# A gated recurrence with a highway layer behind it: two units' gate values stored as pairs of neighbouring tokens

## The chip, the cores and the metric

The kernel runs on one core of a Trainium2 chip. TensorE (PE, with its weight loads shown apart as PEld), VectorE (DVE), ScalarE (ACT) and GpSimd (POOL) work side by side, each through its own instructions in order; SyncE (SP) issues the loads and stores. The metric is the time of one execution on the device in microseconds (us). A profiled execution also gives a span, from its first to its last instruction.

## The reference

Two layers, one behind the other, over 4 sequences of 6336 tokens with 256 channels (25344 tokens in all):

```python
sig = 1.0 / (1.0 + np.exp(-f_logit))
f = lower_bound + (1.0 - lower_bound) * sig
i = 1.0 - f
for t in range(S):                       # a recurrence along each sequence
    h = f[:, t] * h + i[:, t] * x[:, t]
    y[:, t] = h
# y as (25344, 256) is the x of the second layer:
H = np.maximum(x @ w_h, 0.0)
T = 1.0 / (1.0 + np.exp(-(x @ w_t + b_t)))
out = T * H + (1.0 - T) * x
```

## The kernel before, in words

The tokens are cut into 29 **units** of 256, 512 or 1024 tokens (`parts`: two of 2 blocks of 128, three of 4, twenty-two of 8, one of 4, one of 2). Units 10 and 12, which the change touches, have 8 blocks, so 1024 tokens. A unit is loaded with 128 partitions, each holding 8 neighbouring tokens with their 256 channels in float32. The channels are worked in two halves of 128.

The order of the work is written out by hand: `order` is a list of tokens such as `f10.0v:0`, which are issued one after the other. The letter is the step, the first number the unit, the second the half (or piece), `v` puts a step on DVE that else runs on ACT or POOL, and the number behind the colon is the buffer. Each engine runs its instructions in that order. The steps of one unit are:

- `l`, `x`: loads of the logits and of `x`, 1 MB each for a large unit, from SP's queue.
- `u` (ACT): u = sigmoid(-logit), in float16, one instruction of 128x2048 for a whole unit. `u` is kept as [partition, token, channel], and there are four buffers.
- `b` (POOL, in a few places DVE): `bv` = u * x, bfloat16, for one half of the channels, stored as **pairs**: [partition, pair of tokens, channel, token in the pair], so that two neighbouring tokens of one channel share a 4-byte word. There are eight buffers.
- `i` (PE): `u` turned to channels x tokens, into one PSUM bank (`uT`), by one 128x128 transpose for each of the 8 blocks (float16). The bank is then ordered [token in the partition, partition].
- `f` (ACT, or DVE with `v`): f = 1 + ncc * uT, from PSUM to SBUF in float16. It puts the tokens in their order in time, and so reads the bank with a hop of 128 values at each step. Among the large units only `f10.0` and `f12.1` run on DVE.
- `p` (PE): `bv` turned in the same way, but as 4 transposes of 4-byte words: each word holds a pair. The results are written at a step of 4 words, so that the bank is in the order of time.
- `s` (DVE): the recurrence, one scan of 1024 steps for each half.
- `g`, `z` (PE): the two products with the weights; `t` (ACT): the sigmoid of `z`; `d` (DVE): the maximum, from `y` and `g`; `e` (POOL or DVE): d = d * t.
- `o` (PE): output and transposition back into PSUM; `c` (ACT, sometimes DVE): copy to SBUF; `w`: store from SP's queue.

PSUM banks are shared: slots `a0` and `a1` (one bank each) hold `uT` and `bT` in turn, slots `b0` to `b2` (two banks each) hold `g`, `z` and `op` in turn. A step that fills a bank waits until the step that empties the one before has ended. `shared` adds a wait to a POOL product: it doesn't start before the last DVE product of its kind has ended.

Of the kernel before, what the change touches and what calls it, by code (L numbers as in the profile page):

```python
# [11 lines left out]
FP32 = mybir.dt.float32  # L12
BF16 = mybir.dt.bfloat16
FP16 = mybir.dt.float16
AF = mybir.ActivationFunctionType
# [4 lines left out]
def kernel(  # L20
# [10 lines left out]
    nc = tc.nc  # L31
    B, S, D = x.shape
    assert (B, S, D) == (4, 6336, 256)
    P = 128
    NH = D // P
    NB = 8
# [7 lines left out]
    units, at = [], 0  # L44
# [50 lines left out]
w28.1 c28.0:1 w28.0  # L95
"""

    NU = len(units)
    pool = ctx.enter_context(tc.tile_pool(name="sb", bufs=1))
    ps = ctx.enter_context(tc.tile_pool(name="ps", bufs=1, space=bass.MemoryType.PSUM))  # L100

    st = [dict() for _ in range(NU)]
    once = {}
    pin = tc.keep_in_program_order

    def sb(shape, dtype, name, slot=0):
        return pool.tile(shape, dtype, tag=f"{name}{slot}", name=name)
# [19 lines left out]
    def one_bank(slot, dtype, name):  # L127
        t = ps.tile([P, NB * P], dtype, tag=f"a{slot}", name=name)
        busy(t.bitcast(FP32))
        return t  # L130
# [10 lines left out]
    ident_h = sb([P, P], FP16, "ident_h")  # L141
    make_identity(nc, ident_h)
    ident_f = sb([P, P], FP32, "ident_f")
# [19 lines left out]
    def tokens(n):  # L163
        return units[n][0] * P
# [10 lines left out]
    def shared(ins, gpsimd):  # L175

        if not gpsimd:
            held[:] = [ins]
        elif held:
            tc.add_manual_dep(ins.ins, held.pop().ins.name, mybir.DependencyInfo(  # L180
                mybir.DependencyClass.Sync, mybir.DependencyReason.DATA), reason="shared port")
# [80 lines left out]
    def do_u(n, k, eng, slot):  # L262
        nb = units[n][0]
        u = sb([P, NB, D], FP16, "u", slot)
        pin(nc.scalar.activation(u[:, :nb], st[n]["l"][:, :nb], AF.Sigmoid, scale=-1.0))  # L265
        st[n]["u"] = u

    def do_b(n, h, eng, slot):
        nb = units[n][0]
        bv = sb([P, NB // 2, P, 2], BF16, "bv", slot)  # L270
        own = slice(h * P, (h + 1) * P)
        e = nc.vector if eng else nc.gpsimd
        shared(pin(e.tensor_mul(bv[:, :nb // 2].rearrange("p k d j -> p k j d"),  # L273
                                st[n]["u"][:, :nb, own].rearrange("p (k j) d -> p k j d", j=2),
                                st[n]["x"][:, :nb, own].rearrange("p (k j) d -> p k j d", j=2))), not eng)
        st[n]["bv", h] = bv

    def do_i(n, h, eng, slot):
        uT = one_bank(slot, FP16, "uT")
        for j in range(units[n][0]):  # L280
            pin(nc.tensor.transpose(uT[:, j * P:(j + 1) * P], st[n]["u"][:, j, h * P:(h + 1) * P], ident_h))  # L281
        st[n]["uT", h] = uT

    def do_f(n, h, eng, slot):
        N, nb = tokens(n), units[n][0]
        f = sb([P, NB * P], FP16, "f", slot)
        to = f[:, :N].rearrange("c (p j) -> c p j", j=nb)
        of = st[n]["uT", h][:, :N].rearrange("c (j p) -> c p j", j=nb)
        if eng:
            pin(nc.vector.tensor_scalar(to, of, ncc[:, h:h + 1], 1.0, op0=ALU.mult, op1=ALU.add))  # L290
        else:
            pin(nc.scalar.activation(to, of, AF.Identity, scale=ncc[:, h:h + 1], bias=1.0))  # L292
        st[n]["f", h] = f
# [103 lines left out]
    for token in order.split():  # L397
        token, _, slot = token.partition(":")
# [6 lines left out]
        n, _, k = name[1:].partition(".")  # L405
# [29 lines left out]
```

## Time and profile before

| | before |
|---|---|
| time | 206.22 us, median of 2 runs (205.97 to 206.46) |
| profiled execution | 205.65 us, span 203.9 us |
| instructions | 4594 |
| busy, share of the span | ACT 95%, DVE 94%, PE 92%, POOL 85% |
| moved by DMA | 78.68 MB, mean 386 GB/s |
| granted TensorE clock | 0.996 |

The profile divides the span among engines and groups of instructions; a group has its source line, engine, operation, the names of output and inputs with their shape, the count, the busy time and the mean length of one. Idle time is put down to what ended it. The timeline lists instructions with start and length. On ACT, DVE and POOL an instruction can start before the end of the one ahead of it is recorded, so the spacing of starts is shorter than the lengths.

### The profile page before, as it was taken

How to read it: one execution, taken by the hardware profiler on the slowest of the kernel's cores; microseconds unless marked ns; L12 is line 12 of the kernel's file. 1: busy time of each engine (PE TensorE's matmuls, PEld its weight loads, DVE VectorE, ACT ScalarE, POOL GpSimd, SP SyncE). 2: the span in 40 equal slices, each digit the busy share in tenths (PEclk: the TensorE clock that was granted, in tenths of full speed). 3: DMA queues.
4: the chain of work that ended last, by engine and by line, in shares of the span. 5: the costliest groups of instructions: out<-in, count | busy, mean ns of one | idle time of the engine just before them, and what ended most of it. 6: DMA issues, size and time to landing. Idle time of an engine off the chain costs nothing.

```text
span 203.9 us, 4594 instructions
## 1 busy us (share of the span) xinstructions
PE 187.5 (92%) x1794; PEld 131.9 (65%) x1820; DVE 192.6 (94%) x162; ACT 194.2 (95%) x203; POOL 172.8 (85%) x96
## 2 busy tenths in 40 slices
PE   7888869899999989999999999899999999999991
PEld 2455556566766755786668577667767667786880
DVE  2899989999999999999999999999999999999991
ACT  4899999999999999999999999999999999998991
POOL 3147988989999999999999959999999999788720
PEclk9999999999999999999999999999999999999998
DMA  6999999999999999999999999996999999579696
GB/s 213 367 420 424 416 418 423 409 420 422 418 426 416 423 424 417 420 419 424 417 423 420 427 416 416 427 419 273 336 341 411 420 416 399 209 289 367 272 372 251
DMA packets 16413, 78.68 MB, mean 386 GB/s; under 512 B 1796, under 2 KB 2568, under 8 KB 10760
## 3 DMA queue, kind: packets, MB, share of 16 engines
q1 hardware_dynamic: 16384, 78.39, 95.3%
q8 instruction: 14, 0.23, 0.5%
q14 instruction: 7, 0.06, 0.1%
q10 hardware_dynamic: 8, 0.00, 0.0%
HBM read 52.43 MB, written 25.95 MB: 384 GB/s over the span
## 4 chain that ended last, share of the span: by engine, by line
PE 47%; POOL 13%; ACT 12%; DMA 11%; DVE 7%; issue 5%; SPq 1%; ACTq 0%; POOLq 0%; DVEq 0%
DMA x<-in_x_dram 11%; POOL bv L273 8%; PE op L377 7%; PE op L378 7%; PE z L332 6%; PE g L332 6%; PE uT L281 6%; POOL d L355 6%; PE bT L301 5%; DVE y L320 5%; PE z L112 5%; PE g L112 5%; ACT o L390 4%; ACT t L345 3%; ACT f L292 3%
## 5 line engine op out<-in xcount | busy, mean ns | idle before, releaser
L273 POOL TENSOR_TENSOR bv<-u,x 128x1024 bf16<-128x1024 f16 (+2 forms) x53 | 103.7, 1981 | 15.9 <-DVE d L355 7.7
L320 DVE TENSOR_TENSOR_SCAN y<-f,y,bT 128x1024 bf16<-128x1024 f16 (+5 forms) x56 | 107.4, 1929 | 1.1 <-ACT f L292 0.9
L355 POOL TENSOR_TENSOR d<-d,t 128x512 bf16<-128x512 bf16 (+3 forms) x30 | 68.1, 2279 | 6.3 <-ACT t L345 3.6
L349 DVE SCALAR_TENSOR_TENSOR d<-y,ncc,g 128x1024 bf16<-128x1024 bf16 (+2 forms) x58 | 63.6, 1107 | 0.4 <-issue 0.2
L345 ACT ACTIVATE t<-z,bt 128x1024 bf16<-128x1024 f32 (+2 forms) x58 | 58.5, 1048 | 0.5 <-PE z L112 0.5
L292 ACT ACTIVATE f<-uT,ncc 128x1024 f16<-128x1024 f16 (+2 forms) x55 | 58.1, 1060 | 0.5 <-PE uT L281 0.2
L390 ACT COPY o<-op 128x1024 f32<-128x1024 f32 (+2 forms) x55 | 50.9, 966 | 2.1 <-PE op L378 1.8
L265 ACT ACTIVATE u<-l 128x2048 f16<-128x2048 f32 (+2 forms) x29 | 50.4, 1736 | 1.8 <-DMA l<-in_f_logit_dram 1.7
L378 PE MATMUL op<-ident_b,d 128*128 128x128 bf16 x396 | 49.7, 219 | 1.2 <-DVE d L355 0.9
L377 PE MATMUL op<-diag,y 128*128 128x128 f16 x396 | 50.0, 219 | 0.8 <-DVE d L349 0.3
L378 PEld LDWEIGHTS <-d 128*128 128x128 bf16 x396 | 44.0, 113 | 5.5 <-issue 1.3
L377 PEld LDWEIGHTS <-y 128*128 128x128 bf16 x396 | 44.2, 113 | 2.4
L332 PE MATMUL z<-y,w_sb 128*128 128x512 bf16 (+1 forms) x116 | 39.7, 368 | 0.7 <-DVE d L349 0.2
L332 PE MATMUL g<-y,w_sb 128*128 128x512 bf16 (+1 forms) x112 | 39.3, 367 | 1.0 <-DVE d L349 0.2
L301 PE MATMUL bT<-ident_f,bv 128*128 128x128 f32 x198 | 31.9, 277 | 4.8 <-POOL bv L273 2.3
L281 PE MATMUL uT<-ident_h,u 128*128 128x128 f16 x396 | 31.5, 219 | 2.9 <-DVE y L320 1.5
L281 PEld LDWEIGHTS <-u 128*128 128x128 f16 x396 | 26.5, 98 | 11.8 <-issue 4.7
L332 PEld LDWEIGHTS <-w_sb 128*128 128x128 f16 x232 | 22.2, 98 | 14.8 <-ACT f L292 0.2
L301 PEld LDWEIGHTS bT<-ident_f,bv 128*128 128x128 f32 x198 | 22.6, 141 | 14.1 <-POOL bv L273 5.8
L112 PE MATMUL z<-y,w_sb 128*128 128x512 bf16 x79 | 29.9, 379 | 0.0
L112 PE MATMUL g<-y,w_sb 128*128 128x512 bf16 x76 | 28.8, 379 | 0.1
L112 PEld LDWEIGHTS <-w_sb 128*128 128x128 f16 x176 | 17.2, 98 | 15.2 <-issue 1.4
(35 smaller groups left out, 49.5 us busy)
## 6 DMA issues: line engine op xcount, KB each, us to landing
out_dram<-o SPq DMA_DIRECT2D x48, 512.0 KB, 8.6
l<-in_f_logit_dram SPq DMA_DIRECT2D x22, 1024.0 KB, 14.9
x<-in_x_dram SPq DMA_DIRECT2D x22, 1024.0 KB, 15.0
l<-in_f_logit_dram SPq DMA_DIRECT2D x4, 512.0 KB, 7.2
x<-in_x_dram SPq DMA_DIRECT2D x4, 512.0 KB, 7.3
x<-in_x_dram SPq DMA_DIRECT2D x3, 256.0 KB, 4.2
l<-in_f_logit_dram SPq DMA_DIRECT2D x3, 256.0 KB, 3.3
out_dram<-o SPq DMA_DIRECT2D x2, 256.0 KB, 15.0
```

What stands on the lines that cost most here:

```text
L112: return pe.add_instruction(mybir.InstMatmult(name=nc.get_next_instruction_name(), start_tensor_calc=start, stop_tensor_calc=stop, tile_si ...
L273: shared(pin(e.tensor_mul(bv[:, :nb // 2].rearrange("p k d j -> p k j d"), st[n]["u"][:, :nb, own].rearrange("p (k j) d -> p k j d", j=2), ...
L281: pin(nc.tensor.transpose(uT[:, j * P:(j + 1) * P], st[n]["u"][:, j, h * P:(h + 1) * P], ident_h))
L292: pin(nc.scalar.activation(to, of, AF.Identity, scale=ncc[:, h:h + 1], bias=1.0))
L301: pin(nc.tensor.transpose(words[:, k:k + g * (P - 1) + 1:g], pair, ident_f))
L320: pin(nc.vector.tensor_tensor_scan(y[:, c:e], st[n]["f", h][:, c:e], st[n]["bT", h][:, c:e], 0.0 if fresh else carry[h], op0=ALU.mult, op1 ...
L332: pin(nc.tensor.matmul(p[:, a:e], w, half(n, "y", ki)[:, a:e], start=ki == 0, stop=ki == NH - 1))
L345: pin(nc.scalar.activation(half(n, "t", m), st[n]["z", m][:, :tokens(n)], AF.Sigmoid, bias=bt[:, m:m + 1]))
L349: pin(nc.vector.scalar_tensor_tensor(half(n, "d", m), half(n, "y", m), ncc[:, m:m + 1], st[n]["g", m][:, :tokens(n)], op0=ALU.mult, op1=AL ...
L355: shared(pin(e.tensor_mul(st[n]["d"][:, a:c], st[n]["d"][:, a:c], st[n]["t"][:, a:c])), not eng)
L377: pin(nc.tensor.matmul(o, half(n, "y", h)[:, cols], diag[:, h], start=True, stop=False))
L378: pin(nc.tensor.matmul(o, half(n, "d", h)[:, cols], ident_b, start=False, stop=True))
```

## The change

For units 10 and 12, `u` is stored as pairs of neighbouring tokens, as `bv` is already, and `i` turns it with 4 transposes of 4-byte words in place of 8 of 2-byte values. The bank is then in the order of time, and `f` reads and writes it at step one. The two units get to the pairs in different ways: in unit 10 ACT reads the logits in order and writes `u` at a step of two values; in unit 12 (`across`) ACT writes in order and reads across two tokens, one value of the first, then the same channel of the second, 1 KB further. `b` reads the new `u` accordingly: for unit 10 in the order of before, with `u` at a step of two; for unit 12 it runs over pairs, with `u` and `bv` in order and `x` read across the two tokens. Nothing is changed in `order`, in the buffers or in the other units.

```diff
+    paired, across = (10, 12), (12,)
...
     def do_u(n, k, eng, slot):
         nb = units[n][0]
         u = sb([P, NB, D], FP16, "u", slot)
-        pin(nc.scalar.activation(u[:, :nb], st[n]["l"][:, :nb], AF.Sigmoid, scale=-1.0))
+        to, of = u[:, :nb], st[n]["l"][:, :nb]
+        if n in paired:
+            u = sb([P, NB // 2, D, 2], FP16, "u", slot)
+            to = u[:, :nb // 2]
+            if n in across:
+                of = of.rearrange("p (k j) d -> p k d j", j=2)
+            else:
+                to = to.rearrange("p k d j -> p k j d")
+                of = of.rearrange("p (k j) d -> p k j d", j=2)
+        pin(nc.scalar.activation(to, of, AF.Sigmoid, scale=-1.0))
         st[n]["u"] = u
 
     def do_b(n, h, eng, slot):
@@
-        shared(pin(e.tensor_mul(bv[:, :nb // 2].rearrange("p k d j -> p k j d"),
-                                st[n]["u"][:, :nb, own].rearrange("p (k j) d -> p k j d", j=2),
+        if n in paired and n in across:
+            shared(pin(e.tensor_mul(bv[:, :nb // 2], st[n]["u"][:, :nb // 2, own],
+                                    st[n]["x"][:, :nb, own].rearrange("p (k j) d -> p k d j", j=2))), not eng)
+            st[n]["bv", h] = bv
+            return
+        if n in paired:
+            u = st[n]["u"][:, :nb // 2, own].rearrange("p k d j -> p k j d")
+        else:
+            u = st[n]["u"][:, :nb, own].rearrange("p (k j) d -> p k j d", j=2)
+        shared(pin(e.tensor_mul(bv[:, :nb // 2].rearrange("p k d j -> p k j d"), u,
                                 st[n]["x"][:, :nb, own].rearrange("p (k j) d -> p k j d", j=2))), not eng)
         st[n]["bv", h] = bv
 
     def do_i(n, h, eng, slot):
         uT = one_bank(slot, FP16, "uT")
-        for j in range(units[n][0]):
-            pin(nc.tensor.transpose(uT[:, j * P:(j + 1) * P], st[n]["u"][:, j, h * P:(h + 1) * P], ident_h))
+        if n in paired:
+            words, g = uT.bitcast(FP32), units[n][0] // 2
+            for k in range(g):
+                pair = st[n]["u"][:, k, h * P:(h + 1) * P].rearrange("p d j -> p (d j)").bitcast(FP32)
+                pin(nc.tensor.transpose(words[:, k:k + g * (P - 1) + 1:g], pair, ident_f))
+        else:
+            for j in range(units[n][0]):
+                pin(nc.tensor.transpose(uT[:, j * P:(j + 1) * P], st[n]["u"][:, j, h * P:(h + 1) * P], ident_h))
         st[n]["uT", h] = uT
 
     def do_f(n, h, eng, slot):
@@
         of = st[n]["uT", h][:, :N].rearrange("c (j p) -> c p j", j=nb)
+        if n in paired:
+            to, of = f[:, :N], st[n]["uT", h][:, :N]
```

## The prediction

> **What bounds the kernel now.** I read the shares of busy time first, then the busy time of each engine by stretch, since an average over start, middle and end hides which stage is full.
>
> ```profile
> PE 187.5 (92%) x1794; PEld 131.9 (65%) x1820; DVE 192.6 (94%) x162; ACT 194.2 (95%) x203; POOL 172.8 (85%) x96
> ...
> 30.00:183.00 153.00, 147.57 (x1444) 105.57 (x1463) 152.02 (x103) 152.98 (x142) 145.25 (x65) 1.00 0.98 397
> 183.00:203.90 20.90, 16.13 (x180) 12.06 (x179) 15.93 (x21) 15.09 (x24) 10.12 (x9) 0.96 0.83 317
> ```
>
> The columns of the last two rows are stretch, length, then busy time of PE, PE's weight loads, DVE, ACT, POOL, the granted clock, the DMA share and GB/s. From 30 to 183 us ACT is idle 0.02 us and DVE 0.98 us of 153; POOL is idle 7.75 us. So a microsecond added to ACT in the middle has no hole to fall into, a microsecond taken from DVE helps only if ACT and POOL let it, and POOL has a little room, whose place matters.
>
> Next the timeline, followed by hand from the changed units to the end, because busy shares don't say who waits for whom.
>
> ```profile
> 65.85 2.07 ACT L265 ACTIVATE u<-l 128x2048 f16<-128x2048 f32 x1
> 67.65 1.28 ACT L345 ACTIVATE t<-z,bt 128x1024 bf16<-128x1024 f32 x1
> ...
> 85.84 1.17 ACT L390 COPY o<-op 128x1024 f32<-128x1024 f32 x1
> 87.00 1.11 ACT L292 ACTIVATE f<-uT,ncc 128x1024 f16<-128x1024 f16 x1
> 88.01 1.11 ACT L345 ACTIVATE t<-z,bt 128x1024 bf16<-128x1024 f32 x1
> 89.00 1.02 ACT L390 COPY o<-op 128x1024 f32<-128x1024 f32 x1
> 89.90 1.14 ACT L345 ACTIVATE t<-z,bt 128x1024 bf16<-128x1024 f32 x1
> ...
> 90.40 0.81 PE L332 MATMUL g<-y,w_sb 128*128 128x512 bf16 x2
> ...
> 91.52 1.28 DVE L349 SCALAR_TENSOR_TENSOR d<-y,ncc,g 128x1024 bf16<-128x1024 bf16 x1 [0.24 <-issue]
> ...
> 120.30 2.36 DVE L355 TENSOR_TENSOR d<-d,t 128x2048 bf16<-128x2048 bf16 x2
> ...
> 122.79 2.15 POOL L273 TENSOR_TENSOR bv<-u,x 128x1024 bf16<-128x1024 f16 x1 [2.62 <-DVE d L355]
> ...
> 168.37 4.29 POOL L273 TENSOR_TENSOR bv<-u,x 128x1024 bf16<-128x1024 f16 x2
> 170.67 0.61 PE L301 MATMUL bT<-ident_f,bv 128*128 128x128 f32 x4
> 171.37 2.35 DVE L320 TENSOR_TENSOR_SCAN y<-f,y,bT 128x1024 bf16<-128x1024 f16 x1 [0.30 <-ACT f L292]
> ...
> 186.33 1.01 ACT L390 COPY o<-op 128x1024 f32<-128x1024 f32 x1 [0.82 <-PE op L378]
> ```
>
> Columns: start, length, engine and line; in brackets idle time and its releaser. Matched with the written order, 65.85 is `u12` and 89.00 is `c10.0`. ACT issues back to back, so an instruction costs the spacing of starts (67.65 - 65.85 = 1.80 us for `u12`), less than its length. A copy `c` costs 0.90 (89.00 to 89.90); from 85.84 to 87.00 are 1.16, so **ACT has one hole of 0.26 us**, before `f15.0`. `c10.0` empties the bank that `g13.0` fills, at 90.02; `g13.0` starts at 90.40, and DVE's `d13.0` at 91.52 waits for it. From there DVE is full up to 122.66, the end of `e16.0` and what POOL waits for at 122.79. POOL then runs to 170.52 and PE's four `p25.0` to 171.28; the scan at 171.37 comes right behind them (its row names ACT, but POOL and PE came last). From then DVE is full, and ACT waits in its turn at 186.33. The end thus hangs on **ACT up to 89, DVE to 122.7, POOL to 170.5, DVE to the end**. Units 10 and 12 fall into the first part.
>
> **The change part by part.** The prices of what runs today, from the groups that keep shapes apart (count, busy us, mean ns):
>
> ```profile
> L265 ACT ACTIVATE u<-l 128x2048 f16<-128x2048 f32 x22 | 44.1, 2004 | 0.1
> L265 ACT ACTIVATE u<-l 128x1024 f16<-128x1024 f32 x4 | 4.3, 1071 | 0.2 <-DMA l<-in_f_logit_dram 0.2
> L292 ACT ACTIVATE f<-uT,ncc 128x1024 f16<-128x1024 f16 x42 | 50.4, 1200 | 0.0
> L345 ACT ACTIVATE t<-z,bt 128x1024 bf16<-128x1024 f32 x44 | 50.5, 1190 | 0.5 <-PE z L112 0.5
> L290 DVE TENSOR_SCALAR f<-uT,ncc 128x1024 f16<-128x1024 f16 x2 | 2.5, 1267 | 0.0
> L355 DVE TENSOR_TENSOR d<-d,t 128x1024 bf16<-128x1024 bf16 x4 | 2.7, 681 | 0.1
> L273 POOL TENSOR_TENSOR bv<-u,x 128x1024 bf16<-128x1024 f16 x44 | 94.4, 2169 | 7.8 <-DVE d L355 5.1 <-ACT t L345 1.4 <-DMA x<-in_x_dram 0.8
> L355 POOL TENSOR_TENSOR d<-d,t 128x1024 bf16<-128x1024 bf16 x5 | 10.6, 2137 | 0.0
> L301 PE MATMUL bT<-ident_f,bv 128*128 128x128 f32 x198 | 31.9, 277 | 4.8 <-POOL bv L273 2.3 <-ACT f L292 1.9 <-DVE bv L273 0.4
> L281 PE MATMUL uT<-ident_h,u 128*128 128x128 f16 x396 | 31.5, 219 | 2.9 <-DVE y L320 1.5 <-ACT f L292 0.6 <-DVE f L290 0.5
> L377 PEld LDWEIGHTS <-y 128*128 128x128 bf16 x396 | 44.2, 113 | 2.4
> L281 PEld LDWEIGHTS <-u 128*128 128x128 f16 x396 | 26.5, 98 | 11.8 <-issue 4.7 <-ACT u L265 0.3
> ```
>
> *Transposes.* Four half units take 4 transposes of word pairs in place of 8 of single values. Busy time by count: 8 x 31.5/396 = 0.636 us before, 4 x 31.9/198 = 0.644 after, written as `bT` is written today. Zero. No DMA, wait or queue position changes; only instructions in place.
>
> *`f` on ACT* (`f10.1`, `f12.0`). Today `f` reads the bank with a hop at every value (1200 ns) and `t` reads along (1190). Step one is worth 0.01 us each: zero.
>
> *`f` on DVE* (`f10.0`, `f12.1`). Both are the only large `f` there: 1267 ns. No row shows a 16-bit step-one read of PSUM by DVE. Bounds: 1267, no gain, and 681, the step-one 16-bit product of the same size from SBUF. Both tensors of `f` are then 16-bit and step one like that product's, so I take 681: 0.59 us less each, 1.17 in all, after `f12.1`. Where does it go? ACT's order is full up to 85.84, so ACT gains only where it waited: the hole of 0.26 us at 87.00, behind `i15.0`, which PE reaches behind `z12.0`, which reads DVE's `s12.0`. What is late next is ACT itself: `c10.0` sets `g13.0` and `d13.0`. I count **-0.26**; bounds 0 and -1.17.
>
> *`u10` on ACT.* Same reads; the 2-byte results go to every second place. No row has ACT writing so. POOL's `bv` does (2169 ns) against its step-one `d` (2137): 1.5% for POOL. On ACT the bounds are 0 and every value paid twice: (2004 - 1071)/1024 = 0.91 ns a value, 1.87 us for 2048. I take 0, as POOL's row is near the low end.
>
> *`u12` on ACT.* Writes in order, reads one float of a token, then one 1 KB further on. Bounds again 0 and 1.87 us. The `f` row says hops of 256 bytes cost nothing, but from PSUM; the nearest SBUF read with gaps is the weight load of `y` (every fourth value, 113 ns) against that of `u` (98): 15%. I take 15% of 1.87: **+0.28**, all of it on the path.
>
> [...]
>
> *`b10`* reads `u` at a step of 4 bytes, which `x` has today: zero; bounds as for `b12`.
>
> *`b12`* writes and reads `u` in order, but reads `x` across. POOL's rows give 2.1 us for 1024 values whatever the type. Below, step-one writes can save 0.03. Above, if the whole item is paid twice, +2.1 each. I take 0, the value that both POOL rows sit on. Its cover:
>
> ```profile
> 73.43 8.47 POOL L273 TENSOR_TENSOR bv<-u,x 128x1024 bf16<-128x1024 f16 x4
> 76.71 0.63 PE L301 MATMUL bT<-ident_f,bv 128*128 128x128 f32 x4 [0.63 <-ACT f L292]
> 79.77 0.60 PE L301 MATMUL bT<-ident_f,bv 128*128 128x128 f32 x4
> 81.86 4.09 POOL L355 TENSOR_TENSOR d<-d,t 128x2048 bf16<-128x2048 bf16 x1
> 87.36 0.22 PE L378 MATMUL op<-ident_b,d 128*128 128x128 bf16 x1
> 90.70 2.58 POOL L273 TENSOR_TENSOR bv<-u,x 128x1024 bf16<-128x1024 f16 x1 [0.51 <-PE op L378]
> 113.81 6.36 POOL L273 TENSOR_TENSOR bv<-u,x 128x1024 bf16<-128x1024 f16 x3
> 116.10 0.60 PE L301 MATMUL bT<-ident_f,bv 128*128 128x128 f32 x4
> 116.87 2.34 DVE L320 TENSOR_TENSOR_SCAN y<-f,y,bT 128x1024 bf16<-128x1024 f16 x1
> ```
>
> 8.47/4 = 2.12 us each: `b12.1` ends at 75.55, 1.16 before its transposes; `b12.0` at 77.67, 2.10 before. Behind them wait `b13`, then `e10.0` (ends 85.95, first used 1.41 later); then comes a hole of 0.51. The tight place is `b17.1`: 113.81 + 2.12 = 115.93, transposes 0.17 later, and the scan 0.17 behind these.
>
> **Sum.** -0.26 + 0.28 = +0.02 us. The profiled execution took 205.65 us, its span 203.9 and 1.75 around it; the two runs have a median of 206.22, so that execution lies 0.57 below. I put the change on the median: **206.2 us**.
>
> **Rivals.**
>
> *POOL becomes the bound* (the side of slower). If the reads across make `b12` half as long again, +1.06 each, POOL is 2.12 late behind `b12.0`. `b12` itself still fits (1.16 and 2.10), `e10.0` makes PE 0.71 late, the hole at 90.70 takes 0.51, and `b17.1` comes 1.61 late against 0.34 of room: the scan at 116.87 starts 1.27 late, and DVE, then POOL from 122.79, carry that to the end: 206.2 + 1.3 = 207.5. It decides from 0.85 us on both together (0.51 + 0.34). For it: the hop is 1 KB and no POOL row has one; against: POOL's time hasn't followed the bytes so far. 20%.
>
> [...]
>
> *ACT pays each value of `u12` (or `u10`) twice.* +1.87 at 65.85 (or 45.06), no hole up to `c9.1`, so `c10.0` is late by 1.87 and `g13.0` by that less the 0.38 between 90.02 and 90.40: +1.5 to +1.9, in place of 0.28: 207.4 to 207.9, taken as 207.7. For it: two regions at every value; against: `f`'s row. 13%.
>
> *Both of these:* near 209; with `b12` paid twice (4.2 late, less 0.85 of room: +3.4) beside ACT's 1.9, 211.5. 6%, half of it above 210.3.
>
> *DVE's 1.17 us reach the end.* This needs ACT to be pulled along. Against it: ACT idle 0.02 us in 153. For it: PE is shared, and its order could tighten more waits than the one seen. 206.2 - 1.17 = 205.0, or 205.3 with 0.28 on ACT. 11%.
>
> *The change doesn't do what it says:* DVE's `f` stays at 1267. Then the 0.26 is missing and the time is 206.5, inside the forecast's own range of 205.7 to 206.9. Forecast with this one: 50%.
>
> **Numbers.** The range holds forecast, DVE's rival and both single slower ones: 205.1 to 208.4. What is left out is the 6% of both, and parts of the ends. About 2%, 4.1 us, is what a measurement of this kernel can tell from no change. Faster than 202.1: 1%, no case gives it. Slower than 210.3: 3%, from the last line on both. Within: 96%.
>
> **What would show it.** In the profile after: DVE's two large `f` at 0.68 us (right) or 1.27; ACT's `u12` to the next start at 1.80 to 2.1 us, `u10` at 1.80; POOL's four `b` of units 10 and 12 at 2.12 spacing; transposes of pairs with unchanged spacing; ACT's idle from 30 to 183 still near zero, DVE's up by about a microsecond, since its gain ends in waits. I am wrong if `b12` exceeds 2.5 us, if `u12` passes 2.5, or if DVE's idle stays at 1 us while the time falls by a microsecond.

## The result, and the profile after

| | before | after | after, measured again | a third time |
|---|---|---|---|---|
| time, median (range; executions) | 206.22 (205.97 to 206.46; 2) | 213.41 (213.02 to 213.8; 2) | 208.61 (207.77 to 208.69; 6) | 208.34 (207.73 to 209.82; 8) |
| ratio to the kernel before (95%) | | 1.0349 (1.0253 to 1.0445) | 1.0104 (1.0080 to 1.0128) | 1.0092 (1.0059 to 1.0125) |
| span of the profiled execution | 203.9 | 211.2 | 206.8 | 207.1 |

The prediction was 206.2 us; the first measurement is 213.4. The same kernel later gave 208.3 to 208.6, in 14 executions none above 209.9. The ratios, here and below, leave out executions more than 1.5% above the fastest of their kernel; the medians keep all. So there are two things to explain: about **2 us that the change costs each time** (1.9 to 2.1 by the two later ratios), and some **5 us that come in a few executions**. The first profile shows one of these. That both executions of the first measurement were long and none of the 14 later ones was is not what equal odds in all 16 would give (1 case in 120); why the first measurement differs is not known.

Shares of busy time and the busy time of each engine by stretch, in the changed kernel as first measured; the columns are those of the prediction's rows, the second stretch begins where the end thins out:

```profile
PE 191.5 (91%) x1804; PEld 133.0 (63%) x1804; DVE 197.0 (93%) x162; ACT 195.6 (93%) x203; POOL 173.1 (82%) x96
...
30.00:190.00 160.00, 151.15 (x1456) 107.13 (x1456) 157.37 (x104) 155.27 (x143) 146.27 (x65) 0.99 0.95 380
190.00:211.20 21.20, 15.82 (x174) 11.74 (x172) 15.29 (x21) 14.67 (x24) 9.40 (x9) 0.99 0.80 315
```

ACT, idle for 0.02 us in the middle before, now waits 4.73 of 160; POOL waits 13.73 instead of 7.75. DVE looks full, but that is deceptive, as its groups show (those of the changed shapes and of the products `e`; count, busy us, mean ns):

```profile
L275 ACT ACTIVATE u<-l 128x2048 f16<-128x2048 f32 x22 | 45.6, 2074 | 0.0
L318 ACT ACTIVATE f<-uT,ncc 128x1024 f16<-128x1024 f16 x42 | 51.0, 1214 | 0.4 <-PE uT L305 0.4
L316 DVE TENSOR_SCALAR f<-uT,ncc 128x1024 f16<-128x1024 f16 x2 | 1.5, 736 | 0.0
L284 POOL TENSOR_TENSOR bv<-u,x 128x1024 bf16<-128x1024 f16 x2 | 4.5, 2288 | 0.0
L302 PE MATMUL uT<-ident_f,u 128*128 128x128 f32 x16 | 2.5, 277 | 0.0
L381 DVE TENSOR_TENSOR d<-d,t 128x2048 bf16<-128x2048 bf16 x3 | 8.0, 2695 | 0.0
```

DVE's three whole-unit products `e` took 1215 ns each before and 2695 now, though nothing about them was changed. The timeline of DVE and POOL in the same execution shows which one it is:

```profile
87.71 8.47 POOL L292 TENSOR_TENSOR bv<-u,x 128x1024 bf16<-128x1024 f16 x4
91.61 5.66 DVE L381 TENSOR_TENSOR d<-d,t 128x2048 bf16<-128x2048 bf16 x1
97.19 1.27 DVE L375 SCALAR_TENSOR_TENSOR d<-y,ncc,g 128x1024 bf16<-128x1024 bf16 x1
97.44 2.13 POOL L292 TENSOR_TENSOR bv<-u,x 128x1024 bf16<-128x1024 f16 x1 [1.25 <-DVE d L381]
```

The row at 91.61 is `e11.0`, recorded as busy for 5.66 us. POOL's train of four is `b14.0`, `b14.1`, `b16.1` and `b15.0`, at 2.12 each; it ends at 96.18. `e11.0` ends at 97.27, 1.09 behind it, which is about what it takes alone. **By these times it did not work for 5.66 us: it stood until POOL's train was over.** In the two other long executions that were profiled (below) it ends 1.08 behind the train. Only `b15.1` waits for it by a semaphore (the `shared` wait, 1.25 us); `b16.1` and `b15.0` started and ran as if DVE had not asked. The same place before:

```profile
85.90 4.29 POOL L273 TENSOR_TENSOR bv<-u,x 128x1024 bf16<-128x1024 f16 x2
90.08 1.20 DVE L355 TENSOR_TENSOR d<-d,t 128x2048 bf16<-128x2048 bf16 x1
```

There POOL's pair ends at 90.19, 0.11 behind the start of `e11.0`, and the pause of 0.51 in front of the prediction's row at 90.70 (`b16.1`, 2.58 long) follows. `e11.0` fell into that pause. The row names PE as what ended it, but the load of `x16`, issued at 76.83 and 13.70 us under way, landed at 90.53, and that is what `b16.1` waited for. In the changed kernel POOL comes to `b16.1` only at 91.95, and there is no pause.

What the lost time does to the others shows in the stretch from 91.6 to 97.3 (columns as above), first in this execution, with the stretches ahead of it and behind it:

```profile
30.00:91.60 61.60, 58.11 (x547) 40.50 (x547) 59.97 (x42) 61.60 (x55) 57.99 (x29) 1.00 1.02 420
91.60:97.30 5.70, 3.46 (x24) 1.92 (x22) 5.70 (x3) 5.69 (x5) 4.59 (x3) 1.00 1.02 418
97.30:189.00 91.70, 88.58 (x874) 63.79 (x874) 90.70 (x61) 86.98 (x84) 82.70 (x34) 0.98 0.90 351
```

and then in the changed kernel measured again:

```profile
91.60:97.30 5.70, 5.48 (x45) 3.50 (x44) 5.70 (x5) 5.70 (x7) 5.70 (x4) 1.00 1.01 417
```

The timeline of POOL and DVE in that second execution:

```profile
87.79 11.61 POOL L292 TENSOR_TENSOR bv<-u,x 128x1024 bf16<-128x1024 f16 x5
91.67 1.47 DVE L381 TENSOR_TENSOR d<-d,t 128x2048 bf16<-128x2048 bf16 x1
93.06 1.27 DVE L375 SCALAR_TENSOR_TENSOR d<-y,ncc,g 128x1024 bf16<-128x1024 bf16 x1
```

and of its five POOL products `b16.1` alone, which here is the one that waits:

```profile
92.02 3.13 POOL L292 TENSOR_TENSOR bv<-u,x 128x1024 bf16<-128x1024 f16 x1
```

PE loses 2.02 us there, since the scans and `d` come late. `e11.0` differs by 5.66 - 1.47 = 4.19, `d13.0` behind it starts 97.19 - 93.06 = 4.13 later, and the spans differ by 211.2 - 206.8 = 4.4. So this one instruction accounts for nearly all of the difference between two executions of the same kernel. It asked at the same moment in both, 91.61 and 91.67, with POOL's train begun 3.90 and 3.88 us earlier. The granted clock is 1.00 up to the end of the lost stretch and 0.98 only behind it, so in this execution the lower clock follows the lost time and is not its cause.

### The profile page after: what moved, and what is told of

Same layout as the page of the kernel before. It is cut to its first block, busy times and chain, and to the rows that moved or that the text cites. A ratio compares the mean times of both kernels' runs of the same rounds, so it can differ in the third digit from the quotient of the medians.

```text
span 211.2 us, 4588 instructions
## 1 busy us (share of the span) xinstructions
PE 191.5 (91%) x1804; PEld 133.0 (63%) x1804; DVE 197.0 (93%) x162; ACT 195.6 (93%) x203; POOL 173.1 (82%) x96
## 4 chain that ended last, share of the span: by engine, by line
PE 23%; POOL 11%; DMA 6%; DVE 6%; issue 4%; ACT 1%; SPq 0%; ACTq 0%; POOLq 0%; DVEq 0%
POOL bv L292 7%; DMA out_dram<-o 6%; PE op L404 4%; PE op L403 4%; POOL d L381 4%; DVE y L346 3%; PE z L358 3%; PE g L358 3%; PE bT L327 2%; PE z L113 2%; PE g L113 2%; DVE d L375 2%; PE uT L305 2%; ACT o L416 1%; DVE o L414 0%
## 5 line engine op out<-in xcount | busy, mean ns | idle before, releaser
L292 POOL TENSOR_TENSOR bv<-u,x 128x1024 bf16<-128x1024 f16 (+2 forms) x51 | 99.5, 1971 | 17.3 <-DVE d L381 5.6
L318 ACT ACTIVATE f<-uT,ncc 128x1024 f16<-128x1024 f16 (+2 forms) x55 | 58.7, 1071 | 1.0 <-PE uT L305 0.6
L275 ACT ACTIVATE u<-l 128x2048 f16<-128x2048 f32 (+2 forms) x29 | 51.9, 1789 | 2.2 <-DMA l<-in_f_logit_dram 2.2
L358 PE MATMUL g<-y,w_sb 128*128 128x512 bf16 (+1 forms) x116 | 40.2, 368 | 1.6 <-ACT t L371 0.7
L113 PE MATMUL z<-y,w_sb 128*128 128x512 bf16 x88 | 33.8, 384 | 0.0
L113 PE MATMUL g<-y,w_sb 128*128 128x512 bf16 x88 | 33.3, 379 | 0.0
L327 PEld LDWEIGHTS bT<-ident_f,bv 128*128 128x128 f32 x198 | 23.2, 142 | 13.9 <-POOL bv L292 5.3
L305 PE MATMUL uT<-ident_h,u 128*128 128x128 f16 x364 | 29.5, 221 | 2.6 <-DVE y L346 1.1
L305 PEld LDWEIGHTS <-u 128*128 128x128 f16 x364 | 24.7, 99 | 10.7 <-issue 4.5
```

Source lines behind the costliest of these rows:

```text
L113: return pe.add_instruction(mybir.InstMatmult(name=nc.get_next_instruction_name(), start_tensor_calc=start, stop_tensor_calc=stop, tile_si ...
L327: pin(nc.tensor.transpose(words[:, k:k + g * (P - 1) + 1:g], pair, ident_f))
L358: pin(nc.tensor.matmul(p[:, a:e], w, half(n, "y", ki)[:, a:e], start=ki == 0, stop=ki == NH - 1))
```

## The experiments

Two questions: what are the 2 us, and what lets `e11.0` in or keeps it out? For the second, the first theory was the **pause** (also called lockout): `e11.0` gets in only where POOL stands still for a moment, as it did before. Its rival, the strides, holds that the strided accesses themselves cost all that is lost. Then came the **phase**: what counts is how far ahead of the border, the moment between the end of one POOL product and the start of the next, `e11.0` asks; and the **draw**: at each border it is open which of the two goes on. The order of the kernels below is that of the questions.

### One unit alone

```diff
-    paired, across = (10, 12), (12,)
+    paired, across = (10,), ()          # unit 10 alone
+    paired, across = (12,), (12,)       # unit 12 alone
```

> Only unit 10 stored as pairs. Lockout theory (the loss is one DVE product, e11.0, that is kept out by POOL products standing back to back, because POOL comes some 0.7 us or more later to b16.1 than before and the pause of 0.5 us there is gone): u10 costs ACT about 0.6 us more and POOL 0.45, the pause closes all the same, e11.0 takes 5 to 6 us, and the time is 210.5 to 212.5. Rival (the strided writes and reads cost what is lost, each unit its share): half of the loss, 209 to 210, with e11.0 near 1.2 us.

> Only unit 12 stored as pairs. Lockout theory: u12 costs ACT about 0.5 us more, its two POOL products 0.12 each, POOL reaches b16.1 0.7 us late or more; the pause closes, e11.0 takes 5 to 6 us, 210.5 to 212.5. If POOL is less than 0.4 us late the pause stays and the time is 206.5 to 207. Rival (shares of the strides): 209 to 210, e11.0 near 1.2.

Unit 10 alone: 208.84 us (207.25 to 210.22, 4 executions), ratio 1.0126 (1.0054 to 1.0198), in two pairs, 207.25 and 207.59 beside 210.1 and 210.22. Unit 12 alone: 207.65 (207.22 to 208.13), ratio 1.0073 (1.0047 to 1.0100). In both profiled executions POOL ran through without a pause and `e11.0` still took only 1.20 and 1.45 us. That was against the pause theory. Unit 10 alone was profiled twice more:

> One profile of the kernel with unit 10 alone in pairs. If it is a run of 209.5 us or more: by the lockout theory e11.0 takes 3.3 us or more and POOL's b16.1 has its usual 2.15 us; by the rival (another cause, such as late loads) e11.0 takes 1.2 to 1.5 and the time is lost elsewhere. If it is a run of 207 to 208: e11.0 at 1.2 to 1.5, b16.1 at 3.1.

> The same kernel in a second look, with the same two readings: e11.0 of 3.3 us or more in a run of 209.5 us or more (lockout), or 1.2 to 1.5 with the time lost elsewhere (rival).

They gave 214.03 and 207.39 us. Timeline of POOL and DVE in the first:

```profile
88.94 8.49 POOL L292 TENSOR_TENSOR bv<-u,x 128x1024 bf16<-128x1024 f16 x4
93.13 5.38 DVE L381 TENSOR_TENSOR d<-d,t 128x2048 bf16<-128x2048 bf16 x1
98.68 2.14 POOL L292 TENSOR_TENSOR bv<-u,x 128x1024 bf16<-128x1024 f16 x1 [1.25 <-DVE d L381]
```

and in the second:

```profile
86.50 11.62 POOL L292 TENSOR_TENSOR bv<-u,x 128x1024 bf16<-128x1024 f16 x5
90.67 1.20 DVE L381 TENSOR_TENSOR d<-d,t 128x2048 bf16<-128x2048 bf16 x1
```

Unit 10 alone is enough for the whole of it. The pattern is that of the changed kernel: in the long execution POOL's products keep their 2.12 us and `e11.0` takes 5.38; in the short one `e11.0` takes 1.20 and POOL's `b16.1` is stretched to 3.14, so it is POOL that waits. `e11.0` asked 4.19 and 4.17 us behind the start of the train. (Part of the 214.03 was lost ahead of this: POOL's train starts at 88.94 in the long execution and at 86.50 in the short one. The kernel before, run beside it, took 210.86.)

ACT's rows of that short execution, and then of unit 12 alone, give the price of the two forms of `u` apart:

```profile
44.92 2.70 ACT L275 ACTIVATE u<-l 128x2048 f16<-128x2048 f32 x1
47.33 1.14 ACT L416 COPY o<-op 128x1024 f32<-128x1024 f32 x1
```

```profile
65.93 2.61 ACT L275 ACTIVATE u<-l 128x2048 f16<-128x2048 f32 x1
68.23 1.32 ACT L371 ACTIVATE t<-z,bt 128x1024 bf16<-128x1024 f32 x1
```

From start to start that is 2.41 us for the write at a step of two, 2.30 for the read across, against 1.80 for either before: +0.61 and +0.50. `d13.0` starts later by 0.67 and 0.54, measured from the start of `u10`: ACT's delay reaches it whole.

### POOL behind `e11.0` by the written order

```diff
-b14.1:5 b16.1:6 z12.1:1 ... l17:0 b15.0:7 o10.1:2 ... e11.0v d13.0:0
+b14.1:5 z12.1:1 ... l17:0 o10.1:2 ... e11.0v b16.1:6 b15.0:7 d13.0:0
```

With this order the `shared` wait holds `b16.1` until `e11.0` has ended. Run on the changed kernel, with `b15.0` alone moved, and on the kernel before:

> The change whole, but b16.1 and b15.0 stand behind e11.0 in the written order, so that POOL waits for that DVE product in place of keeping it out. Lockout theory: e11.0 back to 1.2 to 1.7 us, the time 207.3 to 208.7 (the 1.1 us on ACT stay, POOL loses up to 0.8). Rival (strides): the strides are all there, so 212 to 214 as in the changed kernel.

> The change whole, with b15.0 alone behind e11.0 in the written order: one POOL product, not two, stands between. Lockout theory: e11.0 waits for b14.1's rest and b16.1 and takes 3.4 to 3.8 us in place of 5.66, the time 210.5 to 212, about 2 us less than the changed kernel. Rival (strides): 213 to 214.

> The kernel before, no pairs, with b16.1 and b15.0 behind e11.0 in the written order, so that POOL always waits for that product. Draw theory: 206.0 to 207.0 and no run above 208, since the meeting is gone. If the order itself costs much: 207.5 or more. This is also the base for what the pairs cost without the meeting: both pairs with this order took 208.45.

Changed kernel with both behind: 208.45 (208.26 to 208.73, 4), ratio 1.0110 (1.0093 to 1.0127). With `b15.0` alone behind: 208.41 (207.84 to 210.08, 4), 1.0142 (1.0091 to 1.0194); there `e11.0` took 1.45 us in the profiled execution, not the expected 3.4 to 3.8. Kernel before with both behind: 206.54 (206.03 to 207.84, 12), 1.0014 (0.9995 to 1.0032). Timeline of the first:

```profile
87.34 4.26 POOL L292 TENSOR_TENSOR bv<-u,x 128x1024 bf16<-128x1024 f16 x2
91.26 1.43 DVE L381 TENSOR_TENSOR d<-d,t 128x2048 bf16<-128x2048 bf16 x1
92.92 6.39 POOL L292 TENSOR_TENSOR bv<-u,x 128x1024 bf16<-128x1024 f16 x3 [1.31 <-DVE d L381]
```

POOL stands still for 1.31 us, `e11.0` takes 1.43, and the time is that of the changed kernel measured again, 208.34 to 208.61. So the 2 us don't hang on which of the two waits; and on the kernel before the order costs nothing that can be measured. In the 26 executions of the four kernels with both products behind (two more follow below) none lies as much as 2.5 us above the fastest of its kernel; of the 50 executions of the kernels here whose profiles show neither this order nor the pause (`b15.0` alone behind counted among these), 10 do. The kernel before, in its 53 executions beside all these, had three between 210.1 and 210.9 and one of 390.32, none of them profiled; what made these long is not known.

### The kernel before with ACT late, and POOL late too

Idle copies of 128x512 on ACT, one ahead of `u10` and two ahead of `u12`; in the second kernel also an idle fill on POOL ahead of `b12.1`. Nothing reads what they write.

```diff
+    late = {10: 1, 12: 2}
...
+        for _ in range(late.get(n, 0)):
+            pin(nc.scalar.activation(idle_act, zeros, AF.Copy))
...
+        if (n, h) == (12, 1):                 # the second kernel alone
+            pin(nc.gpsimd.memset(idle_pool, 0.0))
```

> No pairs at all: the kernel before with small idle copies on ACT (128x512, about 0.45 us each, one ahead of u10, two ahead of u12; the output isn't touched). Lockout theory: ACT and with it POOL come about as late as in the changed kernel, the pause closes, e11.0 takes 5 to 6 us, 211 to 213. Rival (strides): ACT's 1.4 us alone, 207.3 to 208, e11.0 at 1.2.

> No pairs: the kernel before with three idle copies on ACT, as in the run with ACT late, and one idle clear of 128x256 on POOL (about 0.3 us) ahead of b12.1; the output isn't touched. In the run with ACT late e11.0 asked for its turn 0.01 us before POOL's b14.1 was over, and got it. Phase theory (e11.0 is kept out where it asks some tenths of a us before a POOL product is over and the next POOL product is already free to go): now it asks 0.3 us before, e11.0 takes 5 to 6 us, the time is 211.5 to 213.5, 4 us for 0.3 us of idle work. Rival (a POOL product that is late costs its own time): 208.1 to 208.6, e11.0 at 1.2 to 1.5.

ACT late: 208.11 (207.78 to 209.47, 4), ratio 1.0105 (1.0069 to 1.0142). Both late: 207.49 (207.37 to 212.43, 4), 1.0068 (1.0050 to 1.0086). ACT's rows of the first, from the timeline:

```profile
45.90 0.76 ACT L268 ACTIVATE idle_act<-zeros 128x512 bf16<-128x512 bf16 x1
46.42 2.04 ACT L270 ACTIVATE u<-l 128x2048 f16<-128x2048 f32 x1
...
67.27 1.50 ACT L268 ACTIVATE idle_act<-zeros 128x512 bf16<-128x512 bf16 x2
68.67 1.90 ACT L270 ACTIVATE u<-l 128x2048 f16<-128x2048 f32 x1
```

The copies cost 0.52 and 1.40 us from start to start, 1.92 in all, more than the 1.11 of the changed `u`. The time rises by 1.9 and 1.3 us against 206.21 beside them. In the profiles, counted from the start of the first copy, `d13.0` is later than before by 1.76 and 1.70 us. **Lateness of ACT alone, at these two places and with nothing else changed, makes the kernel slower by more than half a microsecond for each of its own.** POOL's delay adds nothing to the measured time (what it does inside is told with the changed kernel, below). In the first, POOL ran its five products without a pause and `e11.0` took 1.20, not the expected 5 to 6. DVE and POOL of the second:

```profile
88.02 11.63 POOL L282 TENSOR_TENSOR bv<-u,x 128x1024 bf16<-128x1024 f16 x5
91.96 1.44 DVE L364 TENSOR_TENSOR d<-d,t 128x2048 bf16<-128x2048 bf16 x1
```

No pause here either, and asked 0.3 us ahead of a border, as in the 213 us execution, `e11.0` got in. That was against the phase as well. The one execution of 212.43 has no profile.

### The kernel before without its pause

The pause at 90.2 ended when the load `x16` had landed. Its issue is moved ahead of a store:

```diff
-o9.1:1 w7.0 t11.1 ... g12.1:1 x16:4 l18:5
+o9.1:1 x16:4 w7.0 t11.1 ... g12.1:1 l18:5
```

> The kernel before with the load of x16 issued ahead of the store w7.0, some 4 us earlier, so that the pause of 0.5 us that POOL makes at b16.1 goes. Pause theory (e11.0 got in only because POOL paused): e11.0 takes 5 to 6 us, 210 to 212, slower though a wait is gone. Phase theory: e11.0 asks 0.03 us before b14.1 is over, gets its turn at the border between two products, 206 to 207 in most runs.

> One profile of the kernel before with the load of x16 early. In a run of 209.5 us or more: e11.0 at 3.3 us or more (lockout), or 1.2 to 1.5 with the time lost elsewhere (rival). In a run of 205 to 207: e11.0 at 1.2 to 1.5.

> The same kernel in a second look, with the same two readings.

Median 206.87 (205.31 to 211.43, 10), ratio 1.0006 (0.9977 to 1.0035), but with three executions at 209.98, 210.2 and 211.43. The two further profiled executions: 207.08 and 210.44. Timeline of POOL and DVE in the second:

```profile
86.45 8.51 POOL L273 TENSOR_TENSOR bv<-u,x 128x1024 bf16<-128x1024 f16 x4
90.64 5.40 DVE L355 TENSOR_TENSOR d<-d,t 128x2048 bf16<-128x2048 bf16 x1
```

and of the first:

```profile
86.27 11.62 POOL L273 TENSOR_TENSOR bv<-u,x 128x1024 bf16<-128x1024 f16 x5
90.44 1.20 DVE L355 TENSOR_TENSOR d<-d,t 128x2048 bf16<-128x2048 bf16 x1
```

This kernel has none of the change in it, only the pause is gone; and it shows the same wait, 5.40 us, in one execution and none in another, asked 4.19 and 4.17 us behind the start of the train. So the layout of `u` is no part of the mechanism. What the change does is to bring POOL to that place later, when there is nothing left to pause for. Without the pause `e11.0` is mostly let in (1.20 to 1.48 us in ten profiles of the kernels here), and sometimes it isn't (5.38 to 5.66 us in three).

### The meeting by itself

A kernel that computes nothing of the reference: POOL runs 60 products of `b`'s shape back to back, DVE runs 24 products of `e`'s shape, each behind two or three copies from PSUM.

```python
for n in range(60):
    pin(nc.gpsimd.tensor_mul(bv[n % 4]..., u..., v...))
for n in range(24):
    for k in range(2 + n % 2):
        pin(nc.vector.tensor_copy(o[(n + k) % 4], z))
    pin(nc.vector.tensor_mul(e[n % 4], d, t))
```

> No part of the reference is computed: 60 POOL products in the form of bv stand back to back, all free to go, while DVE does 24 products of 128x2048 in the form of e, each behind 2 or 3 copies from PSUM, so that they ask at changing points of a POOL product. Draw theory: the DVE products fall in groups, some taking 1.2 us plus the rest of the running POOL product (1.2 to 3.3 us), some 2.1 or 4.2 us more than that; POOL products that had to wait take 3.2. If DVE is always let in at the next border: all between 1.2 and 3.4 us. If a ready POOL train always wins: DVE's first product waits for the whole train, 100 us or more.

The products of both, with least, middle and greatest length in ns:

```profile
L62 DVE TENSOR_TENSOR e<-d,t x24: 1658/1849/2977, 8.3 to 126.9; 128x2048 bf16<-128x2048 bf16 x24
```

```profile
L56 POOL TENSOR_TENSOR bv<-u,v x60: 2126/2139/3128, 2.6 to 149.5; 128x1024 bf16<-128x1024 f16 x60
```

All 24 were let in at the next border: a product that waited through one whole POOL product would be over 2.13 + 1.20 = 3.33 us long, and the longest is 2.98. The POOL product that then waits takes 3.13, as `b16.1` does in the short executions. So an even draw at every border, wherever DVE asks, is out: 24 of 24 here, against two lost borders in a row in each of three profiles above. But the points at which DVE asked did not change as they were meant to. Its timeline repeats itself:

```profile
17.31 2.98 DVE L62 TENSOR_TENSOR e<-d,t 128x2048 bf16<-128x2048 bf16 x1
20.21 3.47 DVE L61 COPY o<-z 128x1024 f32<-128x1024 f32 x3
23.61 1.85 DVE L62 TENSOR_TENSOR e<-d,t 128x2048 bf16<-128x2048 bf16 x1
25.38 2.34 DVE L61 COPY o<-z 128x1024 f32<-128x1024 f32 x2
27.64 2.98 DVE L62 TENSOR_TENSOR e<-d,t 128x2048 bf16<-128x2048 bf16 x1
```

There are only three lengths, 1.66 once, 1.85 twelve times and 2.98 eleven times, and each belongs to one distance ahead of the border (0.53, 0.72 and 1.86 us). In the kernels above that have neither the pause nor the guarding order `e11.0` asks 0.01 to 0.37 us ahead, which this test never tried. There, equal distances came out both ways (the pairs of one kernel above). What decides is **not settled**.

### Giving ACT its time back on DVE

```diff
-f10.1:2 ... f12.0:1          # on ACT
+f10.1v:2 ... f12.0v:1        # on DVE
```

Both kernels here also have `b16.1` and `b15.0` behind `e11.0`; the second has the pairs in unit 12 alone, and `f12.0v` alone.

> A version meant to be faster: the change whole, b16.1 and b15.0 behind e11.0, and f10.1 and f12.0 on DVE too, where a step-one f takes 0.73 us. ACT loses two f of 1.00 us spacing and keeps 1.1 us of u10 and u12: 0.9 us less than before; DVE pays 4 x 0.66 for 2 x 1.19: 0.26 us more. Lockout theory: 206 to 207.5, e11.0 at 1.2 to 1.5. Rival (strides): above 211.

> A version meant to be faster: pairs in unit 12 alone, f12.0 on DVE as f12.1 is, b16.1 and b15.0 behind e11.0. ACT pays 0.5 us more for u12 and saves an f of 1.00: 0.5 less; DVE saves 0.53 on f12.1 and pays 0.66: 0.13 more; POOL 0.24 more. If ACT's time counts in full: 205.5 to 206.3. If DVE's f12.0 comes where DVE holds others up, as f10.1 did on DVE in the version with four: 207 to 208.

Both units, with `f10.1` and `f12.0` on DVE: 210.25 (209.11 to 210.37, 4), ratio 1.0192 (1.0160 to 1.0225). Unit 12 alone, with `f12.0` on DVE: 208.16 (207.25 to 208.78, 6), 1.0091 (1.0064 to 1.0119). Timeline of the first:

```profile
58.76 0.75 DVE L316 TENSOR_SCALAR f<-uT,ncc 128x1024 f16<-128x1024 f16 x1 [1.70 <-PE uT L302]
```

`f10.1` is cheap on DVE, but stands in the order behind an `i10.1` that PE reaches late, and DVE waits 1.70 us for it. Unit 12 alone doesn't gain either (207.65 without). No version here beats the kernel before.

### The changed kernel again

By the draw, executions of this kernel lie partly at 207.5 to 209 us and partly at 211 to 214.

> The changed kernel once more, in more runs. So far two runs gave 213.0 and 213.8 with e11.0 at 5.66 us, while five kernels with the same meeting of e11.0 and b16.1 gave their turn to DVE in the profiled run. [...] Rival (the kept-out product is fixed by the order and the times of this kernel): all runs 212.5 to 214.

> The changed kernel a third time. Draw theory: most runs at 207.5 to 208.8, some at 210 to 214, in two groups. If the first two runs were of another cause than a draw (a chip, a day): all at 207.5 to 208.8.

The times stand in the table at the top. The draw as expected here fails: no execution is in the long group. 12 of the 14 lie at 207.5 to 208.8, as expected if the first two executions were long for a reason of their own, which stays open. Two rows of ACT in the first of them, from the timeline, carry the cost without the long wait:

```profile
45.43 2.70 ACT L275 ACTIVATE u<-l 128x2048 f16<-128x2048 f32 x1
...
69.19 1.33 ACT L371 ACTIVATE t<-z,bt 128x1024 bf16<-128x1024 f32 x1
```

against the same start before:

```profile
45.06 1.93 ACT L265 ACTIVATE u<-l 128x2048 f16<-128x2048 f32 x1
```

From `u10` to the instruction behind `u12` it is 69.19 - 45.43 = 23.76 us; before, 67.65 - 45.06 = 22.59. That is +1.17. `d13.0` starts 93.06 - 45.43 = 47.63 behind `u10`; before, 46.46: again +1.17. The last copy `c28.0` is later by 1.76 on the same measure. So ACT explains 1.17, and some 0.6 arise between `d13.0` and the end. About half of that is POOL's. By the written order DVE's scan `s16.0` needs PE's transposes `p16.0`, and PE has `o12.1` ahead of these, which needs POOL's product `e12.0`; in this execution PE stood 0.47 us for it:

```profile
103.47 0.24 PE L404 MATMUL op<-ident_b,d 128*128 128x128 bf16 x1 [0.47 <-POOL d L381]
...
107.19 2.35 DVE L346 TENSOR_TENSOR_SCAN y<-f,y,bT 128x1024 bf16<-128x1024 f16 x1
```

How much later each starts than before, counted from `u10` or from the first idle copy, in us:

| | `d13.0` (behind ACT) | POOL's `e12.0` | `s16.0` |
|---|---|---|---|
| changed kernel, measured again | 1.17 | 1.50 | 1.46 |
| unit 12 alone | 0.55 | 0.86 | 0.83 |
| before, ACT late | 1.76 | 1.81 | 1.77 |
| before, ACT and POOL late | 1.70 | 2.01 | 1.96 |

From `s16.0` on DVE is as late as POOL, not as ACT. POOL's own share comes from the longer products `b12` (in the last kernel, from the idle fill). The longer `b10` don't get that far: with unit 10 alone `s16.0` is later by 0.69, `d13.0` by 0.67. The other 0.3 us, behind `s16.0`, were not settled.

## Why the prediction was wrong, point by point

**ACT's `u10`, taken as 0: mis-sized.** It costs +0.61 us. The step took POOL's row (a strided write 1.5% dearer) for an engine that it doesn't stand for. The upper bound of 1.87, each value paid twice, was about three times too high.

**ACT's `u12`, taken as +0.28: mis-sized.** It costs +0.49 to +0.50. The 15% came from PE's weight loads, another engine again. The upper bound of 1.87 was nearly four times too high here.

**The gain of -0.26: not seen.** `f` on DVE did become shorter, 736 ns against 1267 (681 forecast). But the hole stays: in the changed kernel measured again, `f15.0` starts 1.16 us behind the start of the copy ahead of it, as before. DVE's gain ends in its own waits: there, from 30 to 185 us, it is busy 152.42 of 155, so idle 2.58 against 0.98. The rival in which 1.17 us of DVE reach the end is out.

**ACT sets the path: right, and it decided.** The prediction's statement that a microsecond added to ACT in the middle has no hole to fall into is what the idle copies showed. With the right prices for ACT and no gain its own sum would have been +1.1, so 207.3; the measured 208.3 to 208.6 leave about 1 us more, of which 0.6 lie behind `d13.0`, half of them POOL's. These later times lie at the upper edge of the stated range (208.4), but that is luck: the edge was set by reads across half as long again, or by values that ACT pays twice, and neither came.

**POOL's `b10` and `b12`, taken as 0: mis-sized.** `b12` takes 2288 ns against 2166 for the other products, +0.12 each, `b10` 2.36 to 2.40, +0.2 each: 0.6 us in all. The prediction had 0.85 us of room for this, the pause of 0.51 and 0.34 at `b17.1`; yet 0.29 us reached DVE at `s16.0`. The rival of half as long again, +1.06 for each `b12`, didn't come: no run shows that term, and with a read of `x` that hops by 1 KB the product took 2.29 us against 2.17.

**Transposes and `f` on ACT: right at zero.** 16 transposes in 2.5 us, 277 ns each, as forecast; `f` on ACT 1214 against 1200.

**What the sum left out.** The prediction used the pause of 0.51 at 90.70 as slack for POOL and never asked what DVE runs in it. **The step that failed is the cover of `b10` and `b12`**: it followed semaphore waits alone, and the meeting of DVE's `e11.0` with a POOL train is no such wait. What the runs showed in its place: with POOL later, the pause is gone and `e11.0` meets the train. In the long execution it then takes 5.66 us in place of 1.20, and `d13.0` starts 4.13 us later than in the short one. In the short ones the pause was no room either: before, POOL passes 0.51 + 2.58 = 3.09 us between `b14.1` and the end of `b16.1`, and in the changed kernel `b16.1` alone takes 3.13, so `e11.0` costs POOL about 1 us in both. The prediction's own row had the sign of it: 2.58 us at 90.70 for a product that elsewhere takes 2.15. Neither the range's upper end, 208.4, nor the 3% for slower by over 2% came from a case with it. The chain "ACT up to 89, DVE to 122.7" held in the short executions; in the long one POOL's train stands between the two.

That the two hold each other up is read from lengths: 1.20 us for `e11.0` in a pause, 3.13 for a POOL product that finds DVE ahead of it, against 2.12 in a train. In the three long profiles DVE's product stood through two POOL products that started after it had asked, and took 5.38 to 5.66 us. Through what part of the chip they do so, no run shows.

## What to carry to other kernels

Where DVE multiplies two tensors from SBUF while POOL runs products without a gap, look at the length of the DVE product in more than one profile: a length of several times its usual one (here 5.38 to 5.66 us against 1.20) was a wait that no semaphore shows. Look too at a product that is somewhat longer than its like next to a pause (here 2.58 us against 2.15): the pause may already be in use. An order that lets POOL wait for that product is a cheap guard (206.54 against 206.3 us here). And a strided access is priced by a row of the same engine, or else both ends are kept as likely (here ACT paid +0.61 and +0.50 us where rows of POOL and PE had given 0 and +0.28).

## What the runs showed of the hardware

- ACT, 2048 values, float32 to float16: a write at a step of two values cost +0.61 us, a read across two tokens 1 KB apart +0.50, on 1.80 between starts (0.30 and 0.24 ns a value).
- DVE read float16 from PSUM at step one in 736 ns for 1024 values, against 1267 with a hop of 256 bytes.
- POOL, a product of 1024 values: a 4-byte step in the float16 input gave 2.36 to 2.40 us, a read of the float32 input across two tokens 2.29, against 2.17.
- DVE's product of 2048 values took 1.20 us in a pause of POOL, 1.20 to 1.48 when it was let in at a border 0.01 to 0.37 us ahead, 1.66 to 2.98 when it asked 0.53 to 1.86 us ahead, and 5.38 to 5.66 in three profiles, with POOL at its usual pace meanwhile.
- Two executions of one program, in which the same instruction asked at 91.61 and 91.67 us, had spans 4.4 us apart.
